# Two zero stores leave the last load of V and join the dwo tiles at the end

## The chip, the cores and the metric

The kernel runs on one core of a Trainium2 chip. The metric is device time in microseconds (us) of one execution, the median of several runs. The core has a matrix engine (TensorE, PE in the profile; PEld is its weight load), VectorE (DVE), ScalarE (ACT), GpSimd (POOL) and SyncE (SP). The last two matter here as issuers: SP and POOL each put transfers between device memory (HBM) and on-chip memory (SBUF) into a queue of their own, and both queues are carried by the same 16 DMA engines.

## The reference

The kernel computes one decode step of a layer and all of its gradients. For 4 batch rows of width 512:

```
xn  = layernorm(x)
q   = xn @ wq                              # 32 heads of 128, 8 KV heads
p   = softmax(q k^T / sqrt(128))           # over the last 1024 of 4096 cached positions
out = x + (p v) @ wo + (gelu(xn @ w_gate) * (xn @ w_up)) @ w_down
```

Returned are `out` and the gradients by x, k_cache, v_cache, wq, wo, w_gate, w_up and w_down for a given `grad_out`, all bf16. The gradients of the two caches, out_2 (K) and out_3 (V), have the caches' full shape, 4 x 8 x 4096 x 128. Attention sees only the last 1024 positions, so in both outputs the first 3072 positions of each head are **zeros that still have to be written**: 50.3 MB of the 81.0 MB that the kernel writes.

## The kernel before

**Zeros.** A tile of zeros, `ztile`, lies in SBUF. `ztodo` (L248) lists 32 stores of 1.5 MB each, two heads of one cache gradient per store, and `zeros(n, after, deep=3)` (L255 to L265) takes the next n off the list. All go through SP's queue, in list order. Each waits for the third zero store before it to land (so at most three are in flight), and, if `after` is given, for that instruction: a load that has landed, or an operation of ACT or DVE that is done. SP does nothing else after the first loads; its last two instructions are the 4 KB stores of `out` and dx. In the text z1 to z32 are the zero stores in list order. Where `zeros` is called decides only how many of the list go out at that place: leave two out at one call, and everything later on the list slides by two.

**Calls of `zeros` before the change:** 4 at the start; 2 behind the load of V of batch row 0 and 3 behind K of row 1 (L399, L400); in the loop over batch rows b, 2, 2 and 4 behind the loads of V for rows 1, 2 and 3 (L645) and 3 each behind K of rows 2 and 3 (L653); in the last row, 3 behind `p_done` (the ACT write of the float softmax, L550), 2 behind `o_done` of the forward (the DVE operation of L596), 2 behind `o_done` of the backward; and at the end 2 in the loop that makes dwo (L740). The four behind V of row 3 are z20 to z23, the three behind `p_done` are z24 to z26, those in the dwo loop are z31 and z32.

**The loop over batch rows** (L631 to L656) works out scores and softmax on K and V of a row, then dV of that row (`dvdk(0, b)`) and dK (`dvdk(1, b)`). `dvdk` (L568) lets PE make 16 blocks of 128 x 512 in PSUM, has ACT or DVE copy them (`evac`, L82) into two staging tiles of 1 MB, and POOL stores both (`result`, L112). In the text dv2a and dv2b are the two stores of dV of row 2, dk1a and dk1b those of dK of row 1, and so on. POOL's queue carries these stores and the later loads of K and V.

**Staging tiles.** The pool `stage` (L74) has four. A tile can be filled again when the store that last read it has landed, so the evictions of dK of row 2 wait for dk1a and dk1b, and those of dV of row 3 for dv2a and dv2b.

**The end.** Four tiles of dwo (L732 to L742) and four of dwq (L747 to L755), each of 8 evictions of 128 x 512 and a 1 MB store on POOL's queue, through the same four staging tiles. The order of instructions on each engine is set by the program's planner; the change moves none on PE, DVE, ACT or POOL. SP's order is written out by hand.

Of the kernel before, what the change touches and what calls it, by code (L numbers as in the profile page):

```python
# [18 lines left out]
def kernel(  # L19
# [24 lines left out]
    nc = tc.nc  # L44
# [56 lines left out]
    def stg_tile():  # L101
        return stage.tile([P, 4096], BF16, name="stg", tag="stg")

    def store(eng, out, in_, kind, apart, **kw):

        d = eng.dma_start(out=out, in_=in_, **kw)  # L106
        for k in apart:
            tc.declare_no_dep(d.ins, group=k, reason="stores write disjoint parts of the outputs")
        tc.add_to_no_dep_group(kind, d.ins)
        return d  # L110
# [8 lines left out]
    def bank(name, tag="w", shape=(P, 512), dt=FP32):  # L119
        pool = {"w": ps_w, "x": ps_x}.get(tag, ps_a)  # L120
        return pool.tile(list(shape), dt, name=name, tag=tag)
# [113 lines left out]
    def load_kv(b, k, pool, tag, eng, **kw):  # L235
        d_, src = ((k_t, A_k_cache), (v_t, A_v_cache))[k]
        tl = pool.tile([P, G, J, Dh], BF16, name=tag, tag=tag)
        for hf in range(2):
            hs = slice(hf * G // 2, (hf + 1) * G // 2)
            with tc.high_priority():  # L240
                d = eng.dma_start(out=tl[:, hs].rearrange("p g j d -> p g (j d)"),  # L241
                                  in_=src[b, hs, K0:Sk, :].rearrange("g (m j) d -> m g (j d)", j=J), **kw)
        d_[b] = tl
        return d
# [6 lines left out]
    def behind(ins, other):  # L251
        tc.add_manual_dep(ins, other.name,
                          mybir.DependencyInfo(mybir.DependencyClass.Sync, mybir.DependencyReason.DATA))

    def zeros(n, after=None, deep=3):  # L255

        for _ in range(n):
            og, b, g = ztodo.pop(0)
            z = store(nc.sync, og[b, g:g + ZG, 0:K0, :].rearrange("g (m j) d -> m g (j d)", m=ZP), zsrc, "zeros",
                      ["rest"])  # L260
            if len(zdone) >= deep:
                behind(z.ins, zdone[-deep].ins)
            if after is not None:
                behind(z.ins, after.ins)
            zdone.append(z)  # L265


    if True:
# [68 lines left out]
        for fb in range(FB):  # L337
            c = fb % 4
# [15 lines left out]
        for wi, (wsb, dh, og) in enumerate(((wu_sb, dhu, out_7), (wg_sb, dhg, out_6))):  # L354
# [13 lines left out]
            for ch in range(4):  # L368
# [5 lines left out]
                for k in range(n7):  # L374
                    for r in range(2):
                        c = nm % 4
# [16 lines left out]
    with tc.tile_pool(name="mid", bufs=1, reuse_waits="tile") as mid:  # L393
# [4 lines left out]
        with tc.tile_pool(name="att", bufs=1, reuse_waits="tile") as att:  # L398
# [81 lines left out]
            def refill(k, b):  # L480

                src = D3[k][:].bitcast(BF16).rearrange("p b e (c g i r) -> p b g e c r i", c=NQ, g=2, r=2)
                t_ = bd[k][b % 2]
                for a, q in enumerate(quad):
                    for g2 in range(2):
                        o_ = a * 8 + g2 * 4
                        nc.gpsimd.tensor_copy(out=t_[q, :, :, g2, :, o_:o_ + 4], in_=src[q, b, g2])

            def scores(k, b):

                t_ = bd[k][b % 2]
                ps = bank("sc_ps", ("S", "dP")[k], (P, NJ))
                src = pairs((k_t, v_t)[k][b][:])
                for g2 in range(2):
                    for e in range(2):
                        sc = scratch()
                        t32(sc[:].rearrange("p (c j m) -> p c j m", c=NQ, j=J), src[:, g2:G:2, :, e * Q:(e + 1) * Q], 1024)
                        sb = sc[:].bitcast(BF16).rearrange("p (c n r) -> p c r n", c=NQ, r=2)
                        for r in range(2):
                            for c, q in enumerate(quad):  # L500
                                mm(ps[q, :], t_[:, e, c, g2, r, :], sb[:, c, r, :], g2 == 0 and e == 0 and r == 0,
                                   g2 == 1 and e == 1 and r == 1, (0, Q * c))
                return ps[:]
# [23 lines left out]
            def softmax(S):  # L527
                m = small("m")
                nc.vector.reduce_max(out=m[:], in_=S, axis=AX.X)
                mT_ps = bank("mT_ps", "x", (1, P))  # L530
                nc.tensor.transpose(mT_ps[:], m[:], ident_f[:])
                mx = small("mx", (1, NQ, 8))
                nc.vector.reduce_max(out=mx[:], in_=mT_ps[:].rearrange("o (c a r) -> o c r a", c=NQ, a=4), axis=AX.X)
                mx4 = small("mx4", (1, NQ, 4, 8))
                TS(out=mx4[:], in0=mx[:].unsqueeze(2).broadcast_to([1, NQ, 4, 8]), scalar1=-1.0, scalar2=None, op0=ALU.mult)
                nm_ps = bank("nm_ps", "x", (P, 1))
                mm(nm_ps[:], mx4[:].rearrange("o c a r -> o (c a r)"), one_f[:])
                negm = small("negm")
                nc.vector.tensor_copy(out=negm[:], in_=nm_ps[:])
                E_f = att.tile([P, NJ], FP32, name="E_f", tag="E_f")  # L540
                es = small("es")
                nc.scalar.activation(out=E_f[:], in_=S, func=ACT.Exp, bias=negm[:, 0:1], scale=1.0, accum_out=es[:])
                es_ps = bank("es_ps", "x", (P, 1))
                mm(es_ps[:], rs2_f, es[:])
                rr = small("rr")
                nc.vector.reciprocal(out=rr[:], in_=es_ps[:])
                P_b = att.tile([P, NJ], BF16, name="P_b", tag="P_b")
                nc.scalar.activation(out=P_b[:], in_=E_f[:], func=ACT.Copy, scale=rr[:, 0:1])
                P_f = att.tile([P, NJ], FP32, name="P_f", tag="P_f")
                p_done = nc.scalar.activation(out=P_f[:], in_=E_f[:], func=ACT.Copy, scale=rr[:, 0:1])  # L550
                load["act"] += 1400
                return P_f, P_b, p_done
# [63 lines left out]
            def turn_wq():  # L616

                half = kap.tile([P, 4, 8, C, Q], U32, name="wq_t", tag="ka")
                w = pairs(wq_sb[:])
                for hc in range(8):  # L620
                    src = w[:, :, hc * 256:(hc + 1) * 256].rearrange("p c (k n) -> p c k n", k=8)
                    if hc < 4:
                        dst = half[:, hc].rearrange("p k c n -> p c k n")
                    else:
                        dst = w[:, :, (hc - 4) * 256:(hc - 3) * 256].rearrange("p c (k n) -> p c k n", k=8)
                    t32(dst, src, 1024)
                    wqT.append(dst)
# [3 lines left out]
            for b in range(B):  # L631
                S = scores(0, b)
                if b + 1 < B:
                    dP = scores(1, b)
                    refill(0, b + 1)
                    refill(1, b + 1)
                P_f, P_b, p_done = softmax(S)
                if b == B - 1:
                    zeros(3, p_done)
                    turn_wq()  # L640
                    dP = scores(1, b)
                pT = turned(P_b, 0)
                o_done = odq(0, b, pT)
                if b + 1 < B:
                    zeros((2, 2, 4)[b], load_kv(b + 1, 1, att, "va", nc.gpsimd, single_packet=True))  # L645
                else:
                    zeros(2, o_done)
                dvdk(0, b, spread(P_b, 0), rows[1])
                dS_b = softmax_d(P_f, dP)
                dST = turned(dS_b, 1)  # L650
                o_done = odq(1, b, dST)
                if b + 2 < B:
                    zeros(3, load_kv(b + 2, 0, (kap, att)[b % 2], ("ka", "kb")[b % 2], nc.gpsimd, single_packet=True))  # L653
                elif b == B - 1:
                    zeros(2, o_done)
                dvdk(1, b, spread(dS_b, 1), rows[0])  # L656

        with tc.tile_pool(name="end", bufs=1, reuse_waits="tile") as end:
# [14 lines left out]
            for n in range(KH):  # L673
                t, e, c = n // 8, n // 4 % 2, n % 4
# [16 lines left out]
            for hc in range(8):  # L691
                for k in range(8):
                    for r in range(2):
                        c = nm % 4
# [37 lines left out]
            for t in range(4):  # L732
                stg = stg_tile()
                for e in range(2):
                    for c, q in enumerate(quad):
                        ps = bank("dwo_ps")
                        mm(ps[:], oSP[q, 2 * t + e, :], dy_b[q, :], pos=(Q * c, 0))
                        o_ = (2 * c + e) * D
                        moved = evac(stg[:, o_:o_ + D], ps[:], D)
                        if e == c == t % 2 == 0:  # L740
                            zeros(1, moved)
                result(dwo_v[t], stg[:])  # L742
            for o_, t_ in ((out_0, out_b), (out_1, dx_b)):
# [42 lines left out]
```

## Time and profile before

| | |
|---|---|
| median of 3 runs | 281.53 us (281.18 to 284.32) |
| the profiled execution | 281.97 us, of which the span of the program is 280.0 us |
| moved between HBM and SBUF | 111.96 MB, mean 400 GB/s |
| SP's queue (q1), share of the 16 engines | 57.1%, 66.34 MB |
| POOL's queue (q0), share | 41.6%, 45.35 MB |
| PE, DVE, ACT busy | 67%, 59%, 45% |

The profile is of one execution. Its span begins with the first instruction of the program and ends with the last; the 1.97 us between span and time lie around it. A DMA's "landing" is when the semaphore that tells of its completion has its full count; a share of 1.00 means that all 16 DMA engines were moving packets all the time (packets are counted whole in the slice where they start, so a short slice can show a little more than 1).

### The profile page before, as it was taken

Reading aid. Unit: us, or ns where it says so; the run is one execution under the profiler, and the core shown is the slowest. Engines: PE = TensorE matmul, PEld = TensorE weight load, DVE = VectorE, ACT = ScalarE, POOL = GpSimd, SP = SyncE. Lnnn points to the kernel's source line nnn. Section 1 sums busy time; section 2 is a strip of 40 time slices with the busy share of each in tenths; the row PEclk is TensorE's granted clock in tenths of the full one; section 3 lists DMA queues with packets and bytes.
Section 4 is the critical chain, followed back from the end, with each engine's and each line's share of the span. In section 5 each row is a group of like instructions: output and inputs, shape, how many; then the busy total and the mean of one; then the engine's idle time right before and its main releaser. Section 6 shows DMA issues by size and latency. Waiting matters only on the chain.

```text
span 280.0 us, 4417 instructions
## 1 busy us (share of the span) xinstructions
PE 186.6 (67%) x1733; PEld 75.1 (27%) x1735; DVE 166.1 (59%) x310; ACT 126.2 (45%) x248; POOL 60.3 (22%) x135
## 2 busy tenths in 40 slices
PE   1157998878254998649946652963357997945770
PEld 0012452323123523224311331331034232411110
DVE  7879849888996506435129350475496104497770
ACT  3243775610102487625724402632432768445770
POOL 8500100196282223130040060020020020201110
PEclk9996855559855555555555555555555557775555
DMA  7999989999999999999999999999999999999995
GB/s 277 427 458 436 389 346 427 422 423 416 388 431 429 421 363 381 324 374 427 417 408 379 427 422 423 374 429 427 432 376 423 418 410 393 393 408 410 417 405 241
DMA packets 16755, 111.96 MB, mean 400 GB/s; under 512 B 1360, under 2 KB 1376, under 8 KB 11104
## 3 DMA queue, kind: packets, MB, share of 16 engines
q1 hardware_dynamic: 6552, 66.34, 57.1%
q0 software_dynamic: 10176, 45.35, 41.6%
q8 instruction: 13, 0.21, 0.3%
q14 instruction: 6, 0.05, 0.0%
q10 hardware_dynamic: 8, 0.00, 0.0%
HBM read 30.68 MB, written 81.01 MB: 399 GB/s over the span
## 4 chain that ended last, share of the span: by engine, by line
DMA 37%; PE 26%; DVE 20%; ACT 7%; issue 5%; POOL 2%; POOLq 0%; DVEq 0%; ACTq 0%
DMA out_dram<-stg 16%; DMA va<-in_A_v_cache_dram 13%; DMA kb<-in_A_k_cache_dram 9%; DVE scr L93 6%; PE kv_ps L117 5%; ACT stg L88 5%; PE dwg_ps L117 3%; PE od_ps L117 3%; DVE stg L89 2%; PE ob_ps L117 2%; DVE dqs L611 2%; PE sc_ps L117 2%; DVE wq_sb L93 2%; PE q_ps L117 1%; PE dxq_ps L117 1%
## 5 line engine op out<-in xcount | busy, mean ns | idle before, releaser
L88 ACT CAST stg<-kv_ps 128x512 bf16<-128x512 f32 x118 | 63.7, 604 | 56.6 <-DMA out_dram<-stg 27.7
L106 POOL DMA_DIRECT2D out_dram<-stg x30 | 19.7, 659 | 144.2 <-ACT stg L88 95.9
L117 PE MATMUL sc_ps<-scr,bd 128*32 128x256 bf16 x256 | 24.6, 401 | 21.7 <-DVE scr L93 21.7
L117 PE MATMUL kv_ps<-dm,spr 32*128 32x256 bf16 x128 | 28.9, 399 | 7.4 <-ACT stg L88 5.8
L117 PE MATMUL kv_ps<-qm,spr 32*128 32x256 bf16 x128 | 24.5, 391 | 10.0 <-ACT stg L88 9.6
L93 DVE STREAM_TRANSPOSE scr<-va 128x1024 uint32<-128x1024 uint32 x16 | 18.8, 1215 | 12.7 <-DMA va<-in_A_v_cache_dram 12.6
L117 PEld LDWEIGHTS <-spr 32*128 32x128 bf16 x256 | 12.0, 102 | 46.1 <-issue 41.8
L117 PEld LDWEIGHTS <-bd 128*32 128x32 bf16 x256 | 8.2, 108 | 34.4 <-issue 33.8
L88 ACT CAST stg<-dwg_ps 128x448 bf16<-128x448 f32 x26 | 12.3, 553 | 4.8 <-PE dwg_ps L117 3.9
L88 ACT CAST stg<-dwo_ps 128x512 bf16<-128x512 f32 x18 | 10.0, 588 | 9.8 <-PE dwo_ps L117 9.6
L117 PE MATMUL dwo_ps<-dy_b,oSP 32*128 32x512 bf16 x32 | 9.2, 518 | 6.5 <-ACT stg L88 5.2
L89 DVE CAST stg<-kv_ps 128x512 bf16<-128x512 f32 x10 | 6.6, 679 | 11.5 <-DMA out_dram<-stg 6.3
L93 DVE STREAM_TRANSPOSE scr<-ka 128x1024 uint32<-128x1024 uint32 x8 | 9.6, 1227 | 6.4 <-DMA ka<-in_A_k_cache_dram 4.2
L241 POOL DMA_DIRECT2D va<-in_A_v_cache_dram x8 | 6.0, 756 | 30.9 <-PE od_ps L117 27.1
L93 DVE STREAM_TRANSPOSE scr<-kb 128x1024 uint32<-128x1024 uint32 x8 | 9.8, 1231 | 4.5 <-DMA kb<-in_A_k_cache_dram 3.9
L117 PE MATMUL do_ps<-scr,dyBD 128*128 128x512 bf16 x31 | 10.3, 470 | 2.5 <-DVE scr L93 2.2
L117 PE MATMUL dwq_ps<-dqSP,xn_b 32*128 32x512 bf16 x32 | 10.6, 587 | 2.0 <-ACT stg L88 1.1
L89 DVE CAST stg<-dwq_ps 128x512 bf16<-128x512 f32 x15 | 9.9, 688 | 2.6 <-PE dwq_ps L117 1.9
L596 DVE SCALAR_TENSOR_TENSOR odt<-od_ps,oms,odt 128x128 f32<-128x128 f32 x4 | 1.3, 330 | 17.0 <-ACT odt L595 17.0
L88 ACT CAST stg<-dwq_ps 128x512 bf16<-128x512 f32 x17 | 9.6, 586 | 2.4 <-DMA out_dram<-stg 1.2
L117 PEld LDWEIGHTS <-pT 128*32 128x32 bf16 x256 | 9.2, 140 | 5.2 <-ACT pT L88 2.3
L93 DVE STREAM_TRANSPOSE scr<-wo_sb 128x1024 uint32<-128x1024 uint32 x8 | 9.7, 1233 | 1.2 <-PE do_ps L117 1.2
(203 smaller groups left out, 332.1 us busy)
## 6 DMA issues: line engine op xcount, KB each, us to landing
out_dram<-ztile SPq DMA_DIRECT2D x32, 1536.0 KB, 12.9
out_dram<-stg POOLq DMA_DIRECT2D x24, 1024.0 KB, 12.6
va<-in_A_v_cache_dram POOLq DMA_DIRECT2D x8, 1024.0 KB, 17.2
out_dram<-stg POOLq DMA_DIRECT2D x6, 896.0 KB, 10.6
wq_sb<-in_A_wq_dram SPq DMA_DIRECT2D x1, 4096.0 KB, 23.2
wo_sb<-in_A_wo_dram SPq DMA_DIRECT2D x1, 4096.0 KB, 34.1
kb<-in_A_k_cache_dram POOLq DMA_DIRECT2D x4, 1024.0 KB, 20.8
ka<-in_A_k_cache_dram SPq DMA_DIRECT2D x2, 1024.0 KB, 44.5
```

Source lines behind the costliest of these rows:

```text
L88: return nc.scalar.copy(out=out, in_=in_)
L89: return nc.vector.tensor_copy(out=out, in_=in_)
L93: nc.vector.transpose(out=out, in_=in_)
L106: d = eng.dma_start(out=out, in_=in_, **kw)
L117: nc.tensor.matmul(out, lhsT=lhsT, rhs=rhs, start=first, stop=last, **kw)
L241: d = eng.dma_start(out=tl[:, hs].rearrange("p g j d -> p g (j d)"), in_=src[b, hs, K0:Sk, :].rearrange("g (m j) d -> m g (j d)", j=J), **kw)
L596: done = STT(out=t_[:], in0=ps[:, 1, :], scalar=mk[:, 1:2], in1=t_[:], op0=ALU.mult, op1=ALU.add)
L611: nc.vector.tensor_copy(out=dqs[q, :, :, :, a * B + b], in_=d3v[q])
```

## The change

The call behind the loads of V takes 2 instead of (2, 2, 4): after V of row 3 only z20 and z21 go out. In the dwo loop `zeros(1, moved)` is called in all four tiles instead of in the first and third.

```diff
                 if b + 1 < B:
-                    zeros((2, 2, 4)[b], load_kv(b + 1, 1, att, "va", nc.gpsimd, single_packet=True))
+                    zeros(2, load_kv(b + 1, 1, att, "va", nc.gpsimd, single_packet=True))
                 else:
                     zeros(2, o_done)
...
                         moved = evac(stg[:, o_:o_ + D], ps[:], D)
-                        if e == c == t % 2 == 0:
+                        if e == c == 0:
                             zeros(1, moved)
```

By the list: z22 to z24 now wait for `p_done`, z25 and z26 for the forward's `o_done`, z27 and z28 for the backward's, and z29 to z32 for the first eviction of dwo tiles 0 to 3. The number of stores, their bytes and their order on SP stay.

## The prediction

> **What bounds the kernel now.** I read the page's 40 slices first, then the chain, then the stretch of the change in 1 us steps, and the end last.
>
> ```profile
> DMA  7999989999999999999999999999999999999995
> GB/s 277 427 458 436 389 346 427 422 423 416 388 431 429 421 363 381 324 374 427 417 408 379 427 422 423 374 429 427 432 376 423 418 410 393 393 408 410 417 405 241
> ```
>
> The DMA engines are at nine tenths or more in nearly every slice; q1 and q0 together take 98.7% of the span, while PE is busy for 67%. The bytes don't change, so the time is the time to carry 112 MB plus whatever time the DMA engines stand still. I therefore price the change in DMA idle time, and use the compute engines only to find when transfers become available.
>
> The chain of waits between 160 and 212 us (start, length, what):
>
> ```profile
> 164.18 35.43 DMA out_dram<-stg
> 199.60 0.03 issue
> ...
> 199.70 0.69 DVE stg L89
> ...
> 201.60 2.37 DVE stg L89 x4
> 203.97 0.07 DVE rr L546
> ```
>
> dk1b is issued at 164.18 and lands only at 199.60. Until then the evictions of dK of row 2 have no staging tile: ACT stands still for 7.3 us before 199.63, DVE for 6.3 us. dk1b is slow because zeros share the engines with it. From 194 to 203 us the queues moved:
>
> ```profile
> q1 hardware_dynamic: 259, 2.85, 74.4%
> q0 software_dynamic: 259, 1.00, 27.1%
> ```
>
> Packets alternate one for one (259 each), but a zero store's are 12 KB and dk1b's 4 KB, so POOL's queue gets about a quarter. The same stretch in steps (from:to, length, busy time of PE, PEld, DVE, ACT, POOL, clock, DMA share, GB/s):
>
> ```profile
> 203.00:204.00 1.00, 0.88 (x6) 0.70 (x4) 1.00 (x4) 0.59 (x1) 0.01 (x1) 0.50 0.86 360
> 204.00:205.00 1.00, 0.33 (x2) 0.00 (x0) 1.00 (x2) 0.63 (x2) 0.74 (x1) 0.50 0.84 340
> 205.00:206.00 1.00, 0.41 (x32) 0.30 (x32) 1.00 (x2) 0.84 (x3) 0.75 (x1) 0.50 0.74 295
> 206.00:207.00 1.00, 0.66 (x16) 0.51 (x20) 1.00 (x2) 0.29 (x1) 0.00 (x0) 0.50 1.02 406
> ```
>
> This is the dip to watch: z23 is through, dv2 nearly, and dk2a, issued by POOL at 203.99, brings the share back to 1 at 206.0, 2.0 us after its issue. The dip costs 0.16 + 0.26 = 0.42 us. From 208.5 to 243.5 us the share is 1.01 at 411 GB/s: full. So is the end:
>
> ```profile
> 244.00:277.00 33.00, 19.38 (x66) 4.30 (x65) 23.93 (x42) 18.73 (x35) 4.29 (x8) 0.57 1.00 406
> ```
>
> **The change, part by part.** *Removed at 182 to 204 us:* z22 and z23, two stores of 1.573 MB. From 193.7 to 206.4 us q1 moved 3.17 MB, just these two, and q0 1.95 MB; so from 193.7 on POOL's queue has the engines to itself. z20 and z21 are untouched.
>
> *dk1b lands earlier.* dk1a lands at 190.01 and dk1b at 199.60: 9.6 us for 1.05 MB, at the quarter share. By 194.2 (193.7 and one last 12 KB packet of 0.46 us on each engine) 44% is through; the other 0.59 MB go at the rate of POOL's queue alone, 365 GB/s (1.82 MB from 177.5 to 182.5, q1 empty), in 1.6 us. dk1b lands at **195.8, 3.8 us earlier**. Nothing else holds the evictions: V of row 3 is in by 183.7, its first transposes and the row's K scores are done. So dk2a, 4.39 us behind dk1b's landing, is issued at 200.2, and `p_done` (ACT's L550, 205.26 to 205.76, 6.16 us behind it) comes at 202.0.
>
> *But the DMA runs dry.* POOL's 1.95 MB of dk1 and dv2 need 5.3 us at 365 GB/s: from 193.7 they are gone at 199.0 on average over the engines. No load is left; the next zeros now wait for `p_done`; the next transfer is dk2a, flowing 2.0 us behind its issue, at 202.2. **Idle: 202.2 - 199.0 = 3.2 us**, of which 0.42 was idle before: +2.8. The trace shows no first packet on dry engines, so the 2.0 us is bounded: POOL's dwo0 (issued 250.60) had packets at 252.07, 1.5 us, beside one other store; dk3a (238.25) at 242.7, 4.5 us, under full load of zeros. With 195.8 to 196.3 for dk1b the idle time lies between 2.7 and 6.2 us. I take 2.0, the row with the emptiest engines at this very store.
>
> The Trainium skill ("DMA: Bandwidth & Descriptors", Specifications) gives a first byte after about 1 us on POOL's path and 0.6 us on SP's. By it the idle time would be 2.2 us and the sum 1 us smaller; every issue in this trace took longer, the shortest, z10, 1.26 us.
>
> *Rate.* POOL's 4 KB packets alone move at 365 to 380 GB/s (380 from 233 to 235), beside zeros at some 410 (0.160 us a packet against 0.172): 1.95 MB cost 0.4 us more.
>
> *z22 to z24 behind `p_done`* take the place of z24 to z26, at the same distance from compute; from there to 240 us all repeats 3.8 us earlier. The added wait holds only zeros: SP's queue has nothing else but the two 4 KB stores, which go out behind z32 at about 256 and are long landed at the end.
>
> *Four zeros in the dwo loop* (z31 and z32 before): 3.15 MB more at 411 to 422 GB/s, 7.5 us, against about 4 to 4.5 us by which everything arrives earlier. Here they share with POOL's 8 KB packets (0.318 us), so a dwo store takes eight rounds of 0.46 + 0.32 us, 6.2 us, as long as zeros run. z29 flows from about 244; four zeros, the first beside dk3b, then one dwo store beside each, last to about 268. dwo0 to dwo2 land at about 257, 263 and 269, dwo3 at 271; dwq tiles are refilled as these land, 3.2 us a tile (267.02 to 269.92 to 273.14 before), the last issued at 275.4 and flowing at 277.3. From 268 the queue alone carries dwo3 and dwq0 to dwq2 at 410 GB/s, 2.56 us each, so it gets to the last one at 278.2: DMA stays full, with 0.9 us to spare, and the dips of the end (0.24 us at 274, some 0.15 at 252 to 255) fill: -0.4.
>
> **The sum:** +3.2 - 0.4 (old dip) + 0.4 (rate) - 0.4 (end) = **+2.8 us**. The profiled execution would be 281.97 + 2.8 = 284.8; I set the sum on the median, 281.53, 0.44 below it: 284.3, and add 0.1 because dk1b may land as late as 196.3: **284.4**. This is right at 1% (284.35), about what a measurement of this kernel can tell from no change.
>
> **The rivals.**
> 1. *The stores hide it: no change.* If dv2 and the lagging engines are still draining when dk2a flows, there is no idle time, and only the order of transfers changes: -0.4 + 0.4 + up to 0.7, so 281.1 to 282.2. For it: dk1 and dv2 lag on some engines by several us (counted, as many 4 KB packets as dk1a ends with have started by 183.7, and it lands at 190.0). Against it: lag on some engines is idleness on others. It decides at 202.2: the average engine would need 3 us more work than I count. Chance 0.25.
> 2. *The end is bound by evictions: faster.* The chain's last 30 us are ACT, PE and DVE between stores. If compute set the end, all of it coming 3.8 us earlier would give 277.7. The point from which it decides is DMA slack of 7.5 us in the end; the rows show a share of 1.00 from 244 to 277. Chance 0.04.
> 3. *The staging tiles jam at the end: slower still.* Before, dwq waits 1.2 us for dwo1 beside z32 (chain: 253.44, 10.09 us). With four zeros, dwo2 and dwo3 may land 2 us later on the slowest engine than I count; dwq2 and dwq3 then follow at 3.2 us each and the 0.9 us of spare is gone: +1 to +2 more, 285.5 to 287. Chance 0.16.
> 4. The change does not do what it says, in one respect: z22 and z23 are not what ends up behind dwo, they go to `p_done`. That is counted above and is no case of its own.
>
> **How the numbers follow.** Forecast 0.55, rivals 0.25, 0.04 and 0.16. Low end: the upper end of rival 1, 282.2 (the 1.5 us latency alone gives 283.9); high end: the 4.5 us latency with dk1b at 195.8, 5.7 us idle, 286.9, or a jam, 287.0. Left out are rival 2, some 0.1 of rival 1 and the far end of the jam. Faster by over 1%: 0.04. Within 1%: rival 1's 0.25 and a quarter of the forecast's 0.55 (its low side is under 284.35), and little of the rest: 0.41. Slower: the remaining 0.55.
>
> **What would show it.** dk1b landing near 196 instead of 199.60 and the evictions following at once; a hole in the DMA share between 199 and 202, deeper than the old one, with 1 to 2 slices of the page under 9; z22 issued at about 202; the last dwq store issued near 275 and landing near 281.4. Wrong would be: dk1b not earlier (then q1 was not what held it); a share of 1 through 202 (rival 1); ACT or PE as the last to finish with idle DMA after 260 (rivals 2, 3).

## The result

| | kernel before | changed kernel |
|---|---|---|
| median, first comparison | 281.95 us (4 runs) | 286.21 us (4 runs) |
| ratio, 95% interval | | 1.0123 (1.0078 to 1.0168) |
| median, second comparison | 281.57 us (11 runs) | 284.76 us (6 runs) |
| ratio, 95% interval | | 1.0097 (1.0060 to 1.0134) |
| the profiled execution | 281.97 us | 286.36 us, span 284.5 us |

The change makes the kernel slower by 1.0 to 1.2%, some 2.7 to 3.5 us. Single runs of one and the same kernel scatter by more than that (the kernel before: 280.95 to 284.4 us in 25 runs), so the ratios with their intervals are what to go by; two profiles tell where the time is, and not to a tenth what it costs.

The 40 slices of the changed kernel's page (7.1 us each), DMA share in tenths and GB/s:

```profile
DMA  7999999999999999999999999997499999999996
GB/s 281 433 447 425 373 377 423 431 423 409 392 438 421 420 408 409 385 420 422 395 363 429 428 426 378 361 416 288 154 418 421 416 389 393 404 416 422 411 418 257
```

Two slices that were 9 are now 7 and 4: for part of the time between 192 and 206 us the DMA engines stand still. The GB/s row says the same, 288 and 154 instead of some 420. I call this stretch the hole. Behind it the slices are full again, up to the last one.

The same place in 1 us steps (from:to, length, busy PE, PEld, DVE, ACT, POOL, clock, DMA share, GB/s):

```profile
196.00:197.00 1.00, 0.00 (x0) 0.00 (x0) 0.00 (x0) 0.00 (x0) 0.00 (x0) 0.50 0.91 348
197.00:198.00 1.00, 0.00 (x0) 0.00 (x0) 0.07 (x1) 0.14 (x1) 0.00 (x0) 0.50 0.26 102
198.00:199.00 1.00, 0.50 (x5) 0.21 (x6) 1.00 (x3) 1.00 (x3) 0.00 (x0) 0.50 0.16 66
199.00:200.00 1.00, 1.00 (x7) 0.20 (x5) 1.00 (x2) 1.00 (x2) 0.00 (x0) 0.50 0.09 37
200.00:201.00 1.00, 0.91 (x7) 0.23 (x5) 1.00 (x3) 0.91 (x4) 0.00 (x0) 0.50 0.07 29
201.00:202.00 1.00, 0.88 (x7) 0.62 (x4) 1.00 (x3) 0.73 (x3) 0.00 (x0) 0.50 0.06 25
202.00:203.00 1.00, 0.56 (x2) 0.08 (x1) 1.00 (x3) 0.40 (x1) 0.75 (x1) 0.50 0.02 8
203.00:204.00 1.00, 0.36 (x32) 0.29 (x32) 1.00 (x2) 0.99 (x3) 0.52 (x1) 0.50 0.48 184
204.00:205.00 1.00, 0.47 (x20) 0.33 (x16) 1.00 (x2) 0.37 (x1) 0.23 (x1) 0.50 1.01 385
```

What is missing to 1 adds up to 5.95 us from 196 to 204. From 199 to 202 us the share is 0.09 to 0.06, about one of 16 engines, and from 202 to 203 us it is 0.02. ACT and DVE stood still up to 197.8; from 198 to 202 us DVE is busy all the time and ACT for 0.7 to 1.0 of each microsecond. So the compute does go on earlier, but while it makes dk2 there is nothing to carry.

The chain of waits around it (start, length, what):

```profile
163.68 34.16 DMA out_dram<-stg
197.84 0.03 issue
...
197.93 0.69 DVE stg L89
...
199.84 2.37 DVE stg L89 x4
202.21 0.07 DVE rr L546
```

dk1b lands at 197.84, 1.8 us earlier than before (199.60), and dk2a goes out at 202.22. The end of the span, from 244 to 281 us:

```profile
244.00:281.00 37.00, 17.96 (x56) 3.72 (x54) 22.00 (x38) 16.65 (x30) 4.29 (x8) 0.53 1.01 415
```

A share of 1.01 at 415 GB/s: with four zeros the end is carried without a gap. The last dwq store is issued at 277.05 and lands at 283.03 (273.14 and 278.55 before).

### The profile page after: what moved, and what is told of

Same layout as the page of the kernel before. It is cut to its first block, busy times and chain, and to the rows that moved or that the text cites. A ratio compares the mean times of both kernels' runs of the same rounds, so it can differ in the third digit from the quotient of the medians.

```text
span 284.5 us, 4419 instructions
## 1 busy us (share of the span) xinstructions
PE 184.1 (65%) x1733; PEld 74.1 (26%) x1735; DVE 166.0 (58%) x310; ACT 125.6 (44%) x248; POOL 60.3 (21%) x135
## 4 chain that ended last, share of the span: by engine, by line
DMA 30%; PE 18%; DVE 16%; issue 5%; ACT 3%; POOL 1%; POOLq 0%; DVEq 0%; ACTq 0%
DMA out_dram<-stg 17%; DMA va<-in_A_v_cache_dram 12%; DVE scr L93 7%; PE kv_ps L117 5%; PE od_ps L117 3%; ACT stg L88 2%; PE ob_ps L117 2%; DVE stg L89 2%; DVE dqs L611 2%; PE dwo_ps L117 2%; PE sc_ps L117 2%; DVE wq_sb L93 2%; PE dxq_ps L117 1%; POOL va L241 1%; DVE spr L510 1%
## 5 line engine op out<-in xcount | busy, mean ns | idle before, releaser
L117 PE MATMUL kv_ps<-dm,spr 32*128 32x256 bf16 x128 | 28.0, 391 | 8.5 <-ACT stg L88 6.9
L117 PE MATMUL do_ps<-scr,dyBD 128*128 128x512 bf16 x31 | 9.5, 435 | 2.7 <-DVE scr L93 2.4
L89 DVE CAST stg<-dwo_ps 128x512 bf16<-128x512 f32 x14 | 9.2, 679 | 2.0 <-PE dwo_ps L117 1.9
```

The source lines that it names most:

```text
L89: return nc.vector.tensor_copy(out=out, in_=in_)
L117: nc.tensor.matmul(out, lhsT=lhsT, rhs=rhs, start=first, stop=last, **kw)
```

## The experiments

Theory A: the hole is the cost. The two stores taken away were the work that covered the time between dv2 and dk2; it is lost there, and at the end they still have to be carried at the full rate. Theory B: the four zeros in the dwo loop clog the staging tiles.

### The hole without the longer end

```diff
-                    zeros((2, 2, 4)[b], load_kv(b + 1, 1, att, "va", nc.gpsimd, single_packet=True))
+                    zeros(2, load_kv(b + 1, 1, att, "va", nc.gpsimd, single_packet=True))
...
-                    zeros(3, p_done)
+                    zeros(5, p_done)
```

> z22 and z23 leave the last load of V, as in the change, but wait for p_done together with z24 to z26 (five there); the dwo loop keeps its two zeros. Theory A (the DMA engines stand still because nothing is left to carry between the end of dv2 and dk2, and the time is found again at the end): the same hole of 5 to 6 us in the DMA share near 197 to 203 us and the time of the changed kernel, 3 to 5 us over the kernel before (284.5 to 286.5). Theory B (the four zeros in the dwo loop keep the staging tiles from coming free and the end is what got longer): no loss here, within 1 us of the kernel before.

Measured: 284.21 us against 281.97, ratio 1.0072 (1.0037 to 1.0107). The hole is there. The rows of this kernel, with the same columns:

```profile
195.00:196.00 1.00, 0.00 (x0) 0.00 (x0) 0.55 (x1) 0.62 (x2) 0.00 (x0) 0.50 0.71 291
...
198.00:199.00 1.00, 0.91 (x6) 0.34 (x5) 1.00 (x2) 0.80 (x4) 0.00 (x0) 0.50 0.08 33
...
200.00:201.00 1.00, 0.08 (x1) 0.00 (x0) 1.00 (x2) 0.88 (x2) 0.50 (x1) 0.50 0.00 0
201.00:202.00 1.00, 0.40 (x32) 0.30 (x32) 1.00 (x2) 0.84 (x3) 0.75 (x1) 0.50 0.97 369
202.00:279.00 77.00, 52.93 (x435) 18.50 (x435) 39.23 (x75) 38.80 (x74) 7.33 (x12) 0.54 1.01 409
```

Summed over 194 to 202 us 4.5 us are missing (5 to 6 were expected); from 202 on the share is 1.01. So the loss is there although the dwo loop is as before, which speaks against B; but at 0.7% it is less than the 1.1 to 1.8% (3 to 5 us) that A expected. That left a theory C: the two further zeros in the dwo loop cost something of their own. Both kernels were therefore timed side by side.

> The changed kernel itself, timed beside the next one, and a second profile of it. Theory A (hole alone): the same time as with the two zeros at p_done, within 1 us, since behind the hole both have the same bytes to carry and the DMA engines are full; 1.007 to 1.012 of the kernel before. Theory C (the two further zeros in the dwo loop cost 1 to 1.5 us of their own): 1.010 to 1.014, that much above the next one. In the profile the length of the hole should follow the landing of dk1b: landing plus some 6 us, minus the moment the average DMA engine is done.

> z22 and z23 at p_done, the dwo loop with two zeros, once more, to compare with the changed kernel on the same chip. Theory A: equal to it within 1 us. Theory C: 1 to 1.5 us below it.

The changed kernel took 284.76 us, 1.0097 (1.0060 to 1.0134); this one 285.35 us, 1.0117 (1.0091 to 1.0142). They are equal within what is measured, and the order is turned round. C is out. The four profiles say it more sharply, by the time from dk2a's issue to the landing of the last store (both from the trace):

| | dk2a issued | last landing | between | missing DMA share around the hole |
|---|---|---|---|---|
| changed kernel | 202.22 | 283.03 | 80.81 | 5.95 us |
| changed kernel, second profile | 200.41 | 281.21 | 80.80 | 4.6 us |
| five zeros at `p_done` | 199.75 | 280.51 | 80.76 | 4.5 us |
| the same, second profile | 201.20 | 282.01 | 80.81 | 3.6 us |

Behind the hole there are 11 zero stores and 14 result stores, and they take 80.8 us in whichever order they go. What differs from profile to profile is when dk2a goes out, and that is dk1b's landing plus 4.4 us each time.

The missing share does not order these profiles by their time: the last one has the least, 3.6 us, and at 285.58 us it is the second slowest (the others, in the table's order, 286.36, 284.45 and 283.96). They differ before the change can act. Up to 182 us they run the same instructions as the kernel before, but from 10 to 160 us the kernel before, the changed kernel and the second profile with five zeros moved (first profile of each of the first two, same columns):

```profile
10.00:160.00 150.00, 108.65 (x1058) 45.97 (x1064) 96.90 (x174) 67.88 (x137) 36.30 (x92) 0.59 1.01 404
10.00:160.00 150.00, 106.83 (x1066) 45.45 (x1072) 96.77 (x174) 67.63 (x137) 36.29 (x92) 0.63 1.01 412
10.00:160.00 150.00, 109.06 (x1062) 46.17 (x1068) 96.93 (x174) 67.86 (x137) 36.45 (x92) 0.59 1.01 404
```

8 GB/s over 150 us are 1.2 MB. Part of the lead is left when the hole begins: up to 193.7 us, in the table's order, 78.38, 78.54, 78.79 and 77.82 MB had been moved. A run that is ahead has less left to carry, so its hole is larger, but it ends no sooner, because the end follows dk2a's issue. Both together give the holes: counted from the last row of the table (3.6 us), by the lead at some 410 GB/s and the difference in dk2a's issue, the first three should be 6.0, 4.6 and 4.5 us long, and they are 5.95, 4.6 and 4.5. Like with like, at 404 GB/s, the hole is 3.6 us against the 0.42 us of the kernel before.

### One store moved instead of two

```diff
-                    zeros((2, 2, 4)[b], load_kv(b + 1, 1, att, "va", nc.gpsimd, single_packet=True))
+                    zeros((2, 2, 3)[b], load_kv(b + 1, 1, att, "va", nc.gpsimd, single_packet=True))
...
-                        if e == c == t % 2 == 0:
+                        if e == c == 0 and t < 3:
```

> Only z22's neighbour moves: three zeros stay behind the last load of V, and the dwo loop has three (tiles 0 to 2). Theory A: z22 keeps the engines busy for 3.7 us alone, 5 us beside POOL's stores, so dk1b lands about as late as before and the hole shrinks to 0 to 2.5 us: 0 to 2 us over the kernel before. Theory B: half of the loss of the changed kernel, about 2 us, with no hole in the DMA share.

Measured: 283.69 us, ratio 1.0033 (0.9991 to 1.0076), which fits A's 0 to 2 us and can't be told from no change. The hole in the one profile was not as small as expected: from 200 to 206 us 3.6 us are missing, with dk1b landing at 199.46, hardly earlier than before. This run too is one that was ahead (412 GB/s from 10 to 160 us), which makes its hole larger. The profiled run, 284.07, lies above the median.

### The same stores, released 5.5 us earlier

```diff
-                    zeros((2, 2, 4)[b], load_kv(b + 1, 1, att, "va", nc.gpsimd, single_packet=True))
+                    zeros(2, load_kv(b + 1, 1, att, "va", nc.gpsimd, single_packet=True))
...
-                        evac(sv[c // 2][:, j:j + 2, (c % 2) * 2:(c % 2) * 2 + 2, :], ps[c][:], 512)
+                        moved = evac(sv[c // 2][:, j:j + 2, (c % 2) * 2:(c % 2) * 2 + 2, :], ps[c][:], 512)
+                        if (k, b, j, c) == (1, 2, 0, 2):
+                            zeros(2, moved)
```

> z22 and z23 wait for the first eviction into the staging tile that dk1b frees, instead of the load of V; the dwo loop keeps its two zeros. Theory A: dk1b lands 1.8 to 3.6 us earlier as in the changed kernel, but z22 flows some 2 us behind that landing, so the hole is 2 to 3.5 us instead of 6 and the time is 1 to 3 us over the kernel before. If it is the early restart of the evictions that decides, and not the hole: 2 to 3.5 us under the kernel before. Theory B: no loss.

Measured: 282.53 us, ratio 1.0008 (0.9974 to 1.0042): no change, where A expected 1 to 3 us over the kernel before. This is the run that separates the hole from everything else: it differs from the one with five zeros at `p_done` only in what releases z22 and z23. All its ten runs (280.70 to 283.32 us) lie below all ten of that one (283.44 to 285.91 us) in the same comparison. dk1b lands at 196.20, and z22, waiting for the first eviction into the tile that dk1b frees, is issued at 196.83, 0.6 us behind the landing instead of 6.2:

```profile
196.00:197.00 1.00, 0.14 (x1) 0.10 (x2) 0.71 (x3) 0.78 (x2) 0.00 (x0) 0.50 0.95 381
197.00:198.00 1.00, 1.00 (x7) 0.31 (x6) 1.00 (x2) 1.00 (x3) 0.00 (x0) 0.50 0.80 324
198.00:199.00 1.00, 1.00 (x4) 0.10 (x2) 1.00 (x3) 0.91 (x3) 0.00 (x0) 0.50 1.07 442
199.00:200.00 1.00, 0.91 (x6) 0.49 (x5) 1.00 (x3) 0.80 (x4) 0.00 (x0) 0.50 1.04 434
```

The two stores leave the load of V just as in the change and the evictions restart early, but the hole is 0.25 us, not the 2 to 3.5 us I had expected, and the loss is gone. The run is not one that was ahead (404 GB/s from 10 to 160 us), so the 0.25 us stand against the 3.6 us of the second profile with five zeros. It says a second thing: dk2a goes out at 200.59, 3.4 us sooner than in the kernel before, and the kernel is not faster. The DMA engines were full behind dk2a before as well and have the same bytes to carry, and part of the lead comes back as idle DMA at the end, 1.6 us from 254 to 257 us:

```profile
255.00:256.00 1.00, 0.36 (x4) 0.10 (x2) 0.69 (x1) 0.59 (x1) 0.00 (x0) 0.50 0.43 180
256.00:257.00 1.00, 0.43 (x2) 0.00 (x0) 0.53 (x1) 0.56 (x1) 0.55 (x1) 0.50 0.18 74
```

Just ahead of this ACT had stood still for 8 us, waiting for a staging tile (ACT's row: start, length, line, operation; in brackets the wait):

```profile
250.13 0.59 ACT L88 CAST stg<-dwo_ps 128x512 bf16<-128x512 f32 x1 [8.02 <-DMA out_dram<-stg]
```

The tile is that of dv3b, which landed at 250.05 here and at 240.38 in the kernel before.

### Two more zeros in the dwo loop, none taken away

```diff
-                        if e == c == t % 2 == 0:
+                        if e == c == 0:
```

with the first two stores of the list made a second time when it is used up.

> The zeros of the kernel before stay where they are; the dwo loop has four, so that the first two stores of the list are made a second time, 3.15 MB more to carry, and no hole. Theory A: the end is carried at the full rate of the DMA engines, so it costs what its bytes cost, 7.0 to 7.8 us (288.5 to 289.7). Theory B: the staging tiles jam on top of it, 9 us or more, with DMA share under 1 after 260 us.

Measured: 289.67 us, ratio 1.0259 (1.0187 to 1.0331), that is +7.3 us by the ratio (5.3 to 9.3) and 7.7 us by the medians for 3.15 MB, or 430 and 410 GB/s. The end of this kernel:

```profile
244.00:281.00 37.00, 20.51 (x72) 4.70 (x70) 23.86 (x42) 19.11 (x36) 4.05 (x8) 0.55 1.00 410
```

The share is 1.00 up to 281 us, so there is no jam: B is out by itself, not only by comparison. It is this row that decides; the interval of the time alone would leave B's 9 us possible.

### Two stores left out

```diff
-                    zeros((2, 2, 4)[b], load_kv(b + 1, 1, att, "va", nc.gpsimd, single_packet=True))
+                    zeros(2, load_kv(b + 1, 1, att, "va", nc.gpsimd, single_packet=True))
```

> As the changed kernel, but the dwo loop keeps two zeros and the last two stores of the list are never made, so 3.15 MB of zeros are missing from the output. Theory A: 7.0 to 7.8 us under the changed kernel, what its bytes take at the full rate, but only 3 to 5 us under the kernel before, because the hole eats the rest. Theory C: 8.5 us or more under the changed kernel.

Measured: 278.53 us, ratio 0.9865 (0.9822 to 0.9909). Leaving out 3.15 MB saves 3.8 us against the kernel before (2.6 to 5.0 by the interval), as A expected and about half of the 7.3 us that the same bytes cost where they come on top. The other half, some 3.5 us, is about the size of the hole of a run that is not ahead (3.6 us). The profile of this kernel has 5.85 us missing from 196 to 204 us and is one of those that were ahead (412 GB/s from 10 to 160 us). Against the changed kernel's second time it is 6.2 us, less than the 7.0 to 7.8 expected; from dk2a's issue to the last landing it is 73.42 us against 80.8, 7.4 us.

### The kernel before, a second profile

> The kernel before, for a second profile of it: how far apart do the 16 DMA engines finish dk1b. If the spread is one of the chip's state, it lands again at 198 to 201 us, 8 us or more behind the first engine's part, and the only dip after 190 us is the one near 204, under 1 us.

283.53 us; dk1b lands at 199.00; 15 of the 16 engines have done their part of it between 185 and 194, the last one is 5 us behind them. After 190 us there is a dip near 204, as before, and one of 0.7 us from 254 to 256, which the first profile hardly had. The four microseconds around it:

```profile
253.00:257.00 4.00, 2.06 (x9) 0.31 (x7) 1.98 (x3) 1.75 (x3) 0.55 (x1) 0.50 0.86 352
```

So the expectation of a single dip did not hold. The kernel before waits there for z32, which waits for the first eviction of dwo tile 2, which waits for dk3a's staging tile: dk3a lands at 254.11 here, and landed at 248.89 in the first profile. That gave the last two runs, a search for a version that beats both.

### The end's own dip

```diff
-                        if e == c == t % 2 == 0:
+                        if e == c == 0 and t < 2:
```

on the kernel before, and on the kernel with the stores behind the eviction:

> The kernel before with the second zero of the dwo loop moved from tile 2 to tile 1, everything else as it was. In the kernel before the DMA engines stood still for 0.1 to 1.4 us near 254 us, because z32 waits for the third dwo tile, which waits for dk3's staging tile. If idle time is what costs, this dip goes: 0 to 1.4 us under the kernel before, 0.5 us as a mean. If the order of zeros and result stores in the end matters by itself, it is slower by 1 us or more.

> z22 and z23 behind the first eviction into dk1b's staging tile, and the second zero of the dwo loop at tile 1. Neither hole is left (0.2 us near 197, 1.8 us near 254 without the second edit). If idle time of the DMA engines is the whole cost, 0.5 to 1.5 us under the kernel before (0.995 to 0.998); if an early restart of the evictions is worth something by itself, 2 us or more.

Measured: 282.23 us, 1.0001 (0.9973 to 1.0030), and 282.82 us, 1.0008 (0.9980 to 1.0036). Neither beats the kernel before. In the first one the dip near 254 is gone and turns up behind the zeros instead:

```profile
262.00:268.00 6.00, 5.45 (x19) 1.27 (x17) 5.16 (x8) 5.32 (x10) 1.34 (x3) 0.50 0.72 296
```

PE, ACT and DVE are busy for 5.2 to 5.5 of 6 us here: with no zero left for the end, the result stores come only as fast as the evictions make them. The evictions were late, too: ACT had waited 2.5 us, up to 259.17, for the tile of dk3b, which landed at 259.07 although 15 of its 16 engines were done by 249.1. So the idle place moved, and the time stayed the same.

Of the second one 0.5 to 1.5 us under the kernel before were expected, and they are not there. Its profile has neither dip (shares of 1.01, 1.01 and 0.99 from 190 to 210, to 250 and to 275 us) and at 281.60 us is 0.4 us shorter than that of the kernel before, but its twelve runs as a whole are not shorter. So the idle time seen in a profile does not account for all of the time of the runs; what else there is stays open.

## Why the prediction was right

The direction, the mechanism and the size held: slower by 2.8 us was predicted, 2.7 to 3.5 us is measured in the two ratios, and the medians of 286.21 and 284.76 us lie inside the range. Step by step:

- **dk1b lands earlier: right, over-sized.** Predicted 3.8 us (195.8). The two profiles of the changed kernel have 197.84 and 196.02, those with five zeros at `p_done` 195.36 and 196.81, against 199.60 and 199.00 before: 2.8 us as a mean. The step worked with the mean share of POOL's queue, but a landing needs the last of 16 engines. In the changed kernel's profile 15 engines have done their part of dk1b by 190.0, and one comes at 197.8.
- **The 4.39 us to dk2a and the 6.16 us to `p_done`: right.** dk2a is issued 4.38 us behind dk1b's landing, z22 (204.01) 6.17 us.
- **The hole: right in place and cause, under-sized.** Predicted 3.2 us, bounded by 2.7 and 6.2. The rows show 5.95 and 4.6 us, and 3.6 to 5.9 in the kernels that share it. The term that was off is the moment the engines run dry: 199.0 was predicted, the share is at 0.26 from 197 on. From 193.7 to 203 us POOL's queue moved only 1.41 MB, not the 1.95 MB of the profile before, because more of dv2 was through by then; and the late dk1b makes the other edge later. Most of the first difference is the lead of that run and not the change: the second profile with five zeros, which has no lead, moved 1.94 MB on POOL's queue from 193.7 us up to dk2a's first packets, and its hole is 3.6 us. With its own dk2a (issued 201.20, flowing 1.3 us later) and the predicted 199.0, the prediction's subtraction gives 3.5.
- **dk2a's 2.0 us from issue to full flow: too long.** The share is 0.48 from 203 to 204, which is all engines from about 203.5 on (the trace has dk2a's first packets at 203.53): 1.3 us behind the issue. The Trainium skill ("DMA: Bandwidth & Descriptors", Specifications) gives about 1 us for the first byte on POOL's path; on engines that are dry the row is nearer to that figure than to my 2.0. The prediction also read the trace before wrongly in one place: z10's 1.26 us is not the shortest there, and first packets on empty engines are in it, though on SP's path. The first load, issued by SP at 0.81 us, has packets at 1.85, 1.0 us later.
- **Two more stores at the end cost their bytes, 7.5 us: right.** 7.3 to 7.7 us by time where they come on top, with a wide interval, and 7.4 us from dk2a's issue to the end where they are left out. DMA stays full from 244 to 281 us. The last dwq store was expected at 275.4 and landing at 281.4; it is at 277.05 and 283.03 in the first profile, where dk2a is issued 2.0 us later than predicted, and at 275.19 and 281.21 in the second, where it is 0.2 us later.
- **The sum came out well in part because errors cancel, which is luck.** In the changed kernel's profiles the hole is 1.4 to 2.8 us larger than predicted; what of this is the lead of these runs costs no time. dk1b lands 0.2 to 2.0 us later than predicted, which costs; dk2a flows 0.7 us sooner behind its issue, which gains. And the kernel before has its own dip at the end, hardly visible in the first profile and 0.7 us in the second, which the four zeros close; I had counted 0.4 us.
- **The rivals.** That the stores hide the gap: no, the share falls to 0.02. That evictions bind the end: no, 3.4 us earlier compute gained nothing. The jam: no; its 285.5 to 287 us hold the first median, 286.21, but the share is 1.01 from 244 to 281 us, so the time was not lost there.

What stays open is why single engines lag with dk1b by 8 us and more. In the first profile of the kernel before nine engines are late (194.7 to 199.6, against 188.5 and earlier for the others), in its second profile and in that of the changed kernel one. The Trainium skill ("DMA: Bandwidth & Descriptors", Latency and other measured facts) says that engines 7 and 15 are usually slower, with the cause a guess; a fixed pair does not fit nine late engines in one profile and one in the next of the same kernel, and the trace doesn't number the engines. The scatter of single runs may come from there; that was not tried.

## What to carry to other kernels

Where the DMA engines are full, a transfer is worth its place: taking one out of a stretch that it covers gives back only what is left after the hole, and it has to be paid again in full where it is put. Before a transfer is moved, work out when the queues run dry without it, and what the next transfer waits for; if that wait is the compute which the move was to speed up, the gain turns into idle DMA. Here the same two stores cost nothing that could be measured when they were released by the first eviction, and 0.7 to 1.2% when they were released 5.5 us later, counted from the landing that let the evictions go on.

## What I had not expected of the hardware

One late DMA engine in 16 can hold back a landing for 8 us: in the changed kernel's profile 15 engines were done with dk1b by 190.0 us and the last at 197.8, and the evictions waited for it. By the time they had filled the next store, the other engines had run dry (share 0.09 to 0.06 from 199 to 202 us). And the remaining work took the same time in four profiles, 80.76 to 80.81 us, although two stores of 1.5 MB stood in quite different places of it.
